# A gated linear attention with a maxout FFN: state products in one matmul, sums in quarters, a shorter weight conversion, and new orders

## The chip, the cores and the metric

The kernel runs on one core of one Trainium2 chip. The metric is device time in microseconds (us): the median of the timed runs. A profile of one execution gives a span, from the first to the last instruction. Engines are called as in the profile: PE is TensorE (matmul), PEld its weight loads, DVE VectorE, ACT ScalarE, POOL GpSimd, SP SyncE, which issues most DMAs.

## What is computed

Attention with a complex, data-dependent decay per step, then a feed-forward layer that takes the maximum of three products. Batch 4, 8 heads, 768 steps, head size 48; model width 384, inner width 768; 3072 tokens.

```python
mag = np.sqrt(a_re * a_re + a_im * a_im)
scale = np.minimum(mag, 0.999) / (mag + 1e-06)
a_re_n, a_im_n = (a_re * scale, a_im * scale)
for t in range(S):                                  # S_re, S_im: (B, H, 48, 48)
    new_re = ar * S_re - ai * S_im
    new_im = ar * S_im + ai * S_re
    kv = np.einsum('bhd,bhe->bhde', k[:, :, t], v[:, :, t])
    S_re, S_im = (new_re + kv, new_im)
    y[:, :, t] = np.einsum('bhd,bhde->bhe', q[:, :, t], S_re)
x = y.transpose(0, 2, 1, 3).reshape(3072, 384)
h = np.maximum(np.maximum(x @ w1, x @ w2), x @ w3)
out = h @ w_out
```

q, k, v, a_re and a_im are float32; the four weights are float64 and are turned into float32 on the chip.

## The kernel before

Steps are cut into 24 chunks x of 128 steps of one batch entry; a group g is two chunks (x and y in the lists' names) of two batch entries, 12 groups in all. A chunk is split again into two halves of 64 steps, and heads into odd and even ones, so that head 2i+j stands in partition half j.

The recurrence is solved without a loop over steps. The decay's logarithm (Ln, 128x768 per group) and its angle in turns (w) are formed elementwise by gates (ACT and DVE, some adds by DMA on POOL's queue). Per chunk and on PE: sums are running sums of Ln, cs running sums of the turns, F decays at cut points. ACT turns them into factors (Ek, Eq, En from sums; CS, cosine and sine, from cs; f from F). DVE multiplies k and q by them into uk and uq: per head, 48 cosine rows, a gap of 16, 48 sine rows, 112 in all. PE transposes both (tp), ACT or DVE copies them to K and Q, DVE makes rescaled copies (Q1, Q2, KB, QB, QG), and PE forms the scores A and B, which DVE and ACT pick into atm through masks. dk is the chunk's product of uk with v, which carries the state on (g); y sums atm with v and QG with the state, and is copied to xhx.

The FFN of a group: up multiplies xhx with two 384x768 weights from which w1 was taken off beforehand, so that a maximum with zero and a further maximum give h. The output product is done as seven products of half size (P1 to P7, sums S1 to S4 by DVE; r1, r6, r5, r7, r57, ox, oy add up the result ot), with Px and Py for the part that went through w1. Group 0 has a plain form of its own (up_one, O, o).

Order is written out by hand. SCHEDULE (lines 21 to 125) is a list of steps name:group; the kernel's Bound objects (line 210, the line of nearly every instruction in the profile) chain each engine's instructions in the order in which the list emits them. So each engine works strictly in list order, and what one engine does never changes the order on another. SLOTS names for each PSUM tile one of four slots (0, 2, 4, 6, two banks each); a tile waits for the last reader of its slot's former tile. OTHER holds the steps that go to their second engine: K and Q copies, xhx<-y, absolute values, and relu to DVE instead of ACT.

The parts that the change and the prediction touch:

- weight_step converts one of twelve 128x768 blocks of a weight. The high words of the float64 are read with a step of two. Step a (ACT) takes their absolute value scaled by 2^-112, b (DVE) caps it, c (DVE) shifts it by 3 bits, e (DVE) adds the low word's top 3 bits, f (DVE) puts the sign back in and writes the weight. g takes w1 off, by a DMA or on DVE.
- angles: cs, t, nf, af, sa, sb. cs has four matmuls of 128 rows and 64 weight columns, 192 moving columns, per chunk.
- state: dk has, for each of 8 heads n and half j, a matmul with weight columns 0 to 63 and one with 64 to 111; 64 rows, 48 moving columns. The last chunks of a batch entry do half of the heads.
- seven: r5 and r7 both add to yl: xr = yl + product 5, yl = yl + product 7.
- product: T and t transpose w1 (wt), M multiplies it with w_out (wm); w1 thus becomes part of the output weight. M0 to M2 come before the first up of group 0.

A float32 matmul shows as two records on PE and two weight loads, a transpose as one.

Of the kernel before, what the change touches and what calls it, by code (L numbers as in the profile page):

```python
# [26 lines left out]
turn1:0 Lry:1 sqr:1 t1:0 WL11:0 Lkx:0 tx:0 nfx:0 Wa11:0 Wb10:0 csy:0 afx:0 sax:0 mkx:0 Wb11:0 Wc10:0 Lix:1 sbx:0
uqx:0 sqi:1 Lix:2 Wc11:0 Lky:0 tpqx:0 ty:0 add:1 f3x:0 f2x:0 ukx:0 Fy:0 Qcx:0 We10:0 Wf10:0 nfy:0 tpkx:0 We11:0
lnL:1 WL2:0 Q2x:0 kEnx:0 Eqy:0 expe:1 Eky:0 relu:1 xor:1 expw:1 QBx:0 Kcx:0 abs:1 T2:0 T0:0 t0:0 CL:0 KBx:0 WL1:0
Wa1:0 pw:1 Q1x:0 mky:0 Wb1:0 f0y:0 f1y:0 Wc1:0 t2:0 f2y:0 Wf11:0 lne:1 Lnop:1 Ax:0 g0x:0 Lry:2 g1x:0 We1:0 g2x:0  # L30
half:1 Lqy:0 Cdx:0 f3y:0 Liy:2 Lvx:0 mqy:0 Wa2:0 Wb2:0 lnw:1 expL:1 M0:0 mulw:1 Wc2:0 M1:0 mulai:1 dkx:0 Wf1:0
stt:1 afy:0 say:0 sby:0 Wg1:0 sqi:2 WL4:0 Wa4:0 g3x:0 sumsx:1 Lrx:2 Cdy:0 sqr:2 M2:0 We2:0 QGx:0 atan:1 Wb4:0 Wf2:0
Lvy:0 Eqx:1 Enx:1 Ekx:1 uky:0 Zg:0 tpky:0 h1x:0 m0:0 m1:0 Lkx:2 Z3:0 Wg2:0 Wc4:0 uqy:0 tpqy:0 Lqx:1 Kcy:0 Qcy:0
Bx:0 b0x:0 turn:1 b1x:0 h2x:0 mqx:1 Fx:1 f0x:1 We4:0 f1x:1 Wf4:0 f2x:1 add:2 csx:1 tx:1 yx:0 KBy:0 Q2y:0 nfx:1 xx:0
h3x:0 f3x:1 lnL:2 expe:2 Q1y:0 WL5:0 Wa5:0 Lkx:1 sumsy:1 csy:1 Eky:1 ty:1 Ay:0 kEny:0 Wb5:0 WL7:0 relu:2 mkx:1
g0y:0 Wc5:0 expw:2 U01x:0 nfy:1 abs:2 u01x:0 Lvy:1 We5:0 Eqy:1 Z2:0 g1y:0 Wa7:0 QBy:0 afy:1 Wf5:0 Eny:1 g2y:0 g3y:0
Wb7:0 Wg4:0 U11x:0 xor:2 By:0 dky:0 U02x:0 Lvx:1 b1y:0 h1y:0 b0y:0 QGy:0 yy:0 addw:2 lnw:2 expL:2 xy:0 U11y:0 Wg5:0
u02x:0 U02y:0 afx:1 half:2 u11x:0 Wc7:0 lne:2 We7:0 mulw:2 mulai:2 sbx:1 h2y:0 Z4:0 sax:1 h3y:0 stt:2 atan:2 Wf7:0
U12x:0 u12x:0 say:1 sby:1 Cdy:1 WL8:0 Cdx:1 turn:2 ukx:1 uqx:1 U01y:0 u01y:0 u11y:0 Wa8:0 U12y:0 csy:2 ty:2 u12y:0
csx:2 tpqx:1 tx:2 u02y:0 Qcx:1 nfy:2 Lnop:2 nfx:2 tpkx:1 Fy:1 kEnx:1 Wb8:0 Wc8:0 We8:0 Kcx:1 Wg7:0 Wf8:0 U21y:0  # L40
Wg8:0 KBx:1 f0y:1 u21y:0 Lky:1 Lqy:1 mky:1 afy:2 sumsx:2 dkx:1 Q1x:1 f1y:1 f2y:1 f3y:1 Enx:2 U21x:0 u21x:0 afx:2
# [5 lines left out]
uky:2 Ekx:3 h2y:1 Eqx:3 Enx:3 yy:1 xy:1 Fy:2 f3y:2 h3y:1 dkx:2 f2y:2 abs:3 KBx:2 h0x:2 h1x:2 Q1x:2 f0y:2 f1y:2
U11:1 u11:1 tpky:2 Kcy:2 Lky:3 QBx:2 QGx:2 addw:3 Lqx:3 h2x:2 mqx:3 h3x:2 xor:3 half:3 Cdx:2 tpqy:2 Qcy:2 Q2x:2
lnw:3 kEny:2 expL:3 sumsy:3 Eqy:3 Q2y:2 Eny:3 Lkx:3 mkx:3 Fx:3 Eky:3 U01:1 Ax:2 Q1y:2 J1:0 mulw:3 mulai:3 g0x:2
g1x:2 u01:1 Cdy:2 f3x:3 f2x:3 g2x:2 g3x:2 J2:0 Bx:2 f0x:3 Dx:0 f1x:3 Dy:0 stt:3 KBy:2 h0x:3 U12:1 b0x:2 b1x:2 u12:1  # L50
S3:1 Lvy:2 yx:2 U02:1 QBy:2 Lvx:3 Lry:4 atan:3 turn:3 Liy:4 csy:3 csx:3 Lix:4 Lrx:4 sqr:4 sqi:4 add:4 lnL:4 ty:3
xx:2 By:2 u02:1 Ay:2 S1:1 nfy:3 relu:4 tx:3 expe:4 S2:1 expw:4 P5:1 P6:1 g0y:2 afy:3 say:3 sby:3 nfx:3 sbx:3 g1y:2
afx:3 sax:3 abs:4 dky:2 P1:1 Lqy:3 g2y:2 g3y:2 b1y:2 J4:0 QGy:2 P7:1 Px:1 P2:1 b0y:2 h0y:2 h1y:2 ukx:3 tpkx:3 lne:4
Lnop:4 r1:1 Liy:5 mky:3 h2y:2 h3y:2 S4:1 Kcx:3 uqx:3 yy:2 Lqx:4 kEnx:3 mqy:3 tpqx:3 Qcx:3 P3:1 r6:1 xy:2 Py:1 r5:1
r7:1 P4:1 Fy:3 uky:3 r57:1 f0y:3 f1y:3 xor:4 half:4 oy:1 ox:1 Q1x:3 addw:4 dkx:3 h1x:3 Lvy:3 f2y:3 f3y:3 h0y:3
h2x:3 sumsx:4 Ekx:4 h3x:3 lnw:4 QGx:3 expL:4 Eqx:4 Fx:4 KBx:3 U11:2 Dx:1 QBx:3 mulai:4 Q2x:3 f2x:4 Enx:4 u11:2
Cdy:3 Lkx:4 f1x:4 f0x:4 U01:2 uqy:3 f3x:4 mulw:4 stt:4 atan:4 tpky:3 Kcy:3 Ax:3 g0x:3 mqx:4 g1x:3 Bx:3 g2x:3 g3x:3
b1x:3 b0x:3 u01:2 Cdx:3 turn:4 U02:2 Lrx:5 u02:2 mkx:4 kEny:3 csy:4 csx:4 tx:4 nfx:4 ty:4 nfy:4 yx:3 xx:3 sumsy:4
KBy:3 Eqy:4 Eky:4 Lry:5 S3:2 Eny:4 sqr:5 dky:3 h1y:3 h2y:3 h3y:3 tpqy:3 Qcy:3 Q2y:3 Lix:5 sqi:5 Px:2 afy:4 add:5
lnL:5 expe:5 Dy:1 U12:2 u12:2 S1:2 Py:2 P7:2 Q1y:3 relu:5 lne:5 QBy:3 afx:4 P4:2 Ay:3 By:3 expw:5 S2:2 g0y:3 sbx:4  # L60
abs:5 g1y:3 sax:4 QGy:3 ukx:4 uqx:4 P6:2 P5:2 S4:2 g2y:3 g3y:3 P2:2 P1:2 Lqy:4 r1:2 Liy:6 mqy:4 b1y:3 P3:2 b0y:3
r6:2 r5:2 r7:2 tpkx:4 r57:2 ox:2 oy:2 kEnx:4 tpqx:4 yy:3 xy:3 Fy:4 say:4 Lky:4 sby:4 mky:4 uky:4 Lnop:5 Kcx:4 uqy:4
sumsx:5 xor:5 half:5 U11:3 KBx:4 addw:5 lnw:5 expL:5 mulw:5 Lqx:5 mulai:5 Cdx:4 h0x:4 f2y:4 stt:5 f3y:4 Ekx:5 f0y:4
Lkx:5 Dy:2 Dx:2 Qcx:4 Enx:5 Q1x:4 Cdy:4 u11:3 Eqx:5 QBx:4 mkx:5 Lry:6 QGx:4 Lvx:4 U01:3 Lix:6 atan:5 Q2x:4 u01:3
f1y:4 h0y:4 U02:3 Lrx:6 u02:3 sqr:6 dkx:4 h1x:4 sqi:6 h2x:4 h3x:4 Fx:5 f0x:5 f3x:5 add:6 f1x:5 f2x:5 Ax:4 g0x:4
Lqy:5 g1x:4 Bx:4 lnL:6 expe:6 g2x:4 g3x:4 U12:3 lne:6 b1x:4 tpky:4 turn:5 mqx:5 b0x:4 tpqy:4 Qcy:4 u12:3 Lvy:4
# [5 lines left out]
f1y:5 lnw:6 Lqx:6 h0y:5 u11:4 Q2x:5 expL:6 mulai:6 mulw:6 U01:4 u01:4 tpky:5 h0x:5 Eqx:6 Kcy:5 tpqy:5 stt:6 Ax:5
Lix:7 atan:6 g0x:5 Qcy:5 g1x:5 g2x:5 Bx:5 kEny:5 g3x:5 b0x:5 Q2y:5 U02:4 sqi:7 b1x:5 add:7 lnL:7 relu:7 expe:7
u02:4 U12:4 Fx:6 f2x:6 S3:4 f3x:6 half:6 turn:6 f0x:6 u12:4 Lvy:5 dky:5 h1y:5 Q1y:5 f1x:6 sumsy:6 dkx:5 Eny:6 csy:6
csx:6 h1x:5 mqx:6 S1:4 Dy:3 ty:6 nfy:6 S2:4 Eqy:6 Lqy:6 mqy:6 Eky:6 P1:4 KBy:5 tx:6 nfx:6 afx:6 lne:7 expw:7 afy:6
P7:4 abs:7 Lky:6 Ay:5 QBy:5 g0y:5 g1y:5 g2y:5 yx:5 g3y:5 addw:7 sbx:6 sax:6 ukx:6 uqx:6 By:5 say:6 P5:4 xx:5 P6:4
r1:4 r6:4 r5:4 lnw:7 xor:7 S4:4 half:7 Px:4 P2:4 b0y:5 Py:4 r7:4 P4:4 r57:4 P3:4 expL:7 mulw:7 QGy:5 oy:4 tpqx:6
tpkx:6 b1y:5 Lnop:7 mky:6 Qcx:6 Q1x:6 ox:4 Liy:8 kEnx:6 yy:5 sumsx:7 xy:5 Cdx:6 Enx:7 Fy:6 f2y:6 f0y:6 f3y:6
mulai:7 f1y:6 Eqx:7 QBx:6 QGx:6 Q2x:6 stt:7 Lqx:7 Ekx:7 Lix:8 U01:5 sqi:8 Lry:8 Cdy:6 Kcx:6 Lrx:8 Lvx:6 dkx:6 h1x:6
sby:6 mqx:7 h2x:6 h3x:6 uqy:6 uky:6 sqr:8 add:8 Dy:4 atan:7 turn:7 Ax:6 g0x:6 lnL:8 Lkx:7 expe:8 xor:8 g1x:6 relu:8  # L80
# [962 lines left out]
```

## Time and profile before

| what | value |
|---|---|
| median of 3 runs | 561.72 us (558.76 to 562.83) |
| span of the profiled execution, its only time on record | 556.9 us |
| PE busy | 524.6 us, 94%, 10086 records |
| PEld busy | 449.0 us, 81% |
| DVE busy | 490.4 us, 88%, 770 instructions |
| ACT busy | 370.0 us, 66%, of it 45 table loads 57.7 us |
| POOL busy | 74.4 us, 13% |
| DMA | 49.09 MB, mean 88 GB/s |
| mean granted TensorE clock | 0.988 |

The costliest groups on PE by busy time are up (177.4 us, 792 records), y (39.4 and 38.4), the output products, A (31.6) and dk (25.2 for the 64-column and 22.8 for the 48-column matmuls). Matmuls overlap, so a group's busy time is not what it adds to the span; the chain of waits, which follows the work that ended last, shows that better, with 34% of the span in up, 7% in y, 5% in A and 4% in dk. In the profile's slices a digit is the busy share of an engine in one fortieth of the span, in tenths. A window's row gives busy time by engine with the number of instructions, then the granted clock, the DMA share and GB/s. A group's row gives the engine, the operation, out<-in, the tile of the array where it is one (rows*columns), shapes and count, then busy time, the mean duration in ns, and the idle time in front of it.

### The profile page before, as it was taken

How to read it: one execution, taken by the hardware profiler on the slowest of the kernel's cores; microseconds unless marked ns; L12 is line 12 of the kernel's file. 1: busy time of each engine (PE TensorE's matmuls, PEld its weight loads, DVE VectorE, ACT ScalarE, POOL GpSimd, SP SyncE). 2: the span in 40 equal slices, each digit the busy share in tenths (PEclk: the TensorE clock that was granted, in tenths of full speed). 3: DMA queues.
4: the chain of work that ended last, by engine and by line, in shares of the span. 5: the costliest groups of instructions: out<-in, count | busy, mean ns of one | idle time of the engine just before them, and what ended most of it. 6: DMA issues, size and time to landing. Idle time of an engine off the chain costs nothing.

```text
span 556.9 us, 22739 instructions
## 1 busy us (share of the span) xinstructions
PE 524.6 (94%) x10086; PEld 449.0 (81%) x10086; DVE 490.4 (88%) x770; ACT 370.0 (66%) x652; POOL 74.4 (13%) x117
## 2 busy tenths in 40 slices
PE   1669799989999999999999999999999999999997
PEld 0356588778888898888988888988888888998986
DVE  5999999989998899999988897999999999886524
ACT  5999989867965867787766858777646855530100
POOL 8105250002030001000120200120010020000000
PEclk9869999999999999999999999999999999999999
DMA  8977976456055164235364136542361144000000
GB/s 218 287 191 156 206 154 102 78 105 123 18 108 109 21 123 77 48 63 92 68 115 82 33 61 121 110 88 50 58 126 31 32 88 82 10 31 2 7 25 29
DMA packets 142530, 49.09 MB, mean 88 GB/s; under 512 B 130528, under 2 KB 135648, under 8 KB 142432
## 3 DMA queue, kind: packets, MB, share of 16 engines
q1 hardware_dynamic: 136272, 37.77, 31.9%
q0 software_dynamic: 6160, 9.87, 10.4%
q8 instruction: 79, 1.29, 1.0%
q14 instruction: 19, 0.16, 0.1%
HBM read 33.03 MB, written 4.72 MB: 68 GB/s over the span
## 4 chain that ended last, share of the span: by engine, by line
PE 84%; DVE 6%; DMA 4%; SPq 2%; issue 1%; ACT 1%; POOL 0%; DVEq 0%
PE up L210 34%; PE op L210 24%; PE y L210 7%; PE A L210 5%; PE tp L210 4%; PE dk L210 4%; PE sums L210 3%; PE cs L210 2%; SPq L210 2%; DMA xhx<-in_moe_w_out_dram 2%; PE F L210 2%; DVE xhx L210 1%; PE B L210 1%; DMA k<-in_k_dram 1%; DMA ar<-nf 1%
## 5 line engine op out<-in xcount | busy, mean ns | idle before, releaser
L210 PE MATMUL up<-xhx,w 128*128 128x256 f32 x792 | 177.4, 382 | 0.1
L210 PEld LDWEIGHTS up<-xhx,w 128*128 128x128 f32 x792 | 148.6, 190 | 21.5 <-PE B L210 0.3
L210 ACT ACT_TABLE_LOAD x45 | 57.7, 1283 | 1.5 <-PEq L1027 0.8
L210 ACT COPY atm<-B 32x128 f32<-32x128 f32 x96 | 24.5, 255 | 36.9 <-DVE atm L210 22.9
L210 PE MATMUL op<-wo,xhx 128*128 128x192 f32 (+1 forms) x220 | 48.5, 364 | 0.0
L210 DVE TENSOR_TENSOR Q<-Q,f 112x1024 f32<-112x1024 f32 (+1 forms) x48 | 45.4, 950 | 0.8 <-ACT Q L210 0.6
L210 ACT ACTIVATE f<-F 48x232 f32<-48x232 f32 x96 | 34.4, 359 | 13.2 <-PE F L210 5.4
L210 POOL DMA_DIRECT2D ar<-nf x40 | 34.2, 1280 | 65.3 <-DVE ar L210 54.7
L210 PE MATMUL y<-atm,vb 128*32 128x64 f32 x1152 | 39.4, 221 | 1.4 <-issue 1.1
L210 PEld LDWEIGHTS op<-wo,xhx 128*128 128x128 f32 x220 | 36.5, 190 | 4.3 <-DVE q L210 0.3
L210 POOL DMA_DIRECT2D Ln<-e x11 | 11.1, 1005 | 214.6 <-ACT e L210 53.9
L210 PE MATMUL y<-QG,g 112*32 112x64 f32 x1408 | 38.4, 219 | 0.9 <-issue 0.8
L210 PEld LDWEIGHTS y<-atm,vb 128*32 128x32 f32 x1152 | 32.5, 109 | 6.4 <-issue 3.6
L210 PEld LDWEIGHTS y<-QG,g 112*32 112x32 f32 x1408 | 34.8, 109 | 1.3 <-issue 1.0
L210 DVE TENSOR_TENSOR ot<-ot,op 128x192 f32<-128x192 f32 (+1 forms) x67 | 27.1, 413 | 9.0 <-PE op L210 4.3
L210 PE MATMUL op<-wo,strassen 128*128 128x192 f32 x176 | 33.0, 331 | 0.0
L210 PE MATMUL A<-Q,K 112*32 112x80 f32 x1536 | 31.6, 234 | 1.3 <-DVE Q L210 1.3
L210 DVE COPY_PREDICATED atm<-masko,A 128x256 f32<-128x256 uint8 x72 | 31.2, 435 | 1.6
L210 PE MATMUL op<-w,strassen 128*128 128x192 f32 x176 | 32.5, 329 | 0.0
L210 PEld LDWEIGHTS A<-Q,K 112*32 112x32 f32 x1536 | 27.2, 110 | 5.0 <-issue 1.9
L210 ACT COPY Q<-tp 112x1024 f32<-112x1024 f32 x23 | 23.3, 1013 | 10.3 <-PE tp L210 10.0
L210 ACT COPY ot<-op 128x192 f32<-128x192 f32 (+1 forms) x13 | 4.5, 342 | 38.2 <-PE op L210 38.2
(151 smaller groups left out, 1120.8 us busy)
## 6 DMA issues: line engine op xcount, KB each, us to landing
ar<-in_a_re_dram SPq DMA_DIRECT2D x24, 192.0 KB, 3.7
ai<-in_a_im_dram SPq DMA_DIRECT2D x24, 192.0 KB, 3.8
q<-in_q_dram SPq DMA_DIRECT2D x96, 48.0 KB, 2.6
k<-in_k_dram SPq DMA_DIRECT2D x96, 48.0 KB, 2.9
...
```

Of the source, the lines that this page charges most:

```text
L210: ins = f(*a, **kw)
```

## The change

- Weight conversion: five steps instead of six. b comes first and clamps the signed high word on DVE (two operations in one instruction, read with a step of two, written packed); a is Prelu on ACT in place, with a slope for negative numbers that turns the sign into a bit beyond the shift; c shifts; e adds the low bits and writes the weight. f is gone.
- cs: eight matmuls of 32 weight columns instead of four of 64.
- dk: one matmul of 112 weight columns instead of 64 and 48.
- r5 and r7 become r75, one DVE instruction over both halves, with yl read twice.
- Three ACT biases are numbers instead of columns of a tile.
- Tiles from rotating pools become fixed pairs chosen by chunk; Ek and Eq no longer share theirs.
- SCHEDULE, SLOTS and OTHER are new throughout. On POOL the late constants (CL) move to the front.

```diff
-        if step == "a":
-            activation(out=ex.bitcast(FP), in_=high.bitcast(FP), func=AF.Abs, scale=2.0 ** -112)
-        elif step == "b":
-            dve.tensor_single_scalar(out=ex.bitcast(FP), in_=ex.bitcast(FP), scalar=LAST, op=OP.min)
+        if step == "b":
+            dve.tensor_scalar(out=ex.bitcast(FP), in0=high.bitcast(FP), scalar1=LAST, scalar2=-LAST, op0=OP.min,
+                              op1=OP.max)
+        elif step == "a":
+            activation(out=ex.bitcast(FP), in_=ex.bitcast(FP), func=AF.Prelu, alpha=-2.0 ** 32,
+                       scale=-2.0 ** -112 if i in (0, 3, 6) else 2.0 ** -112)
         elif step == "c":
-            if i in (0, 3, 6):
-                dve.tensor_scalar(out=ex, in0=ex, scalar1=3, scalar2=-0x80000000, op0=OP.logical_shift_left,
-                                  op1=OP.bitwise_or)
-            else:
-                dve.tensor_single_scalar(out=ex, in_=ex, scalar=3, op=OP.logical_shift_left)
+            dve.tensor_single_scalar(out=ex, in_=ex, scalar=3, op=OP.logical_shift_left)
         elif step == "e":
-            dve.scalar_tensor_tensor(out=ex, in0=low, scalar=29, in1=ex, op0=OP.logical_shift_right, op1=OP.bitwise_or)
-        elif step == "f":
-            dve.scalar_tensor_tensor(out=dst.bitcast(I32), in0=high, scalar=-0x80000000, in1=ex,
-                                     op0=OP.bitwise_and, op1=OP.bitwise_xor)
+            dve.scalar_tensor_tensor(out=dst.bitcast(I32), in0=low, scalar=29, in1=ex, op0=OP.logical_shift_right,
+                                     op1=OP.bitwise_or)
...
-                activation(out=e, in_=e, func=AF.Ln, scale=1e-6 * math.exp(-LNMAX), bias=least)
+                activation(out=e, in_=e, func=AF.Ln, scale=1e-6 * math.exp(-LNMAX), bias=math.exp(-LNMAX))
...
             for ch in range(2):
-                for j in range(2):
-                    dst, m = ps[j * L64:(j + 1) * L64, ch * HC:(ch + 1) * HC], slice(ch * L64, (ch + 1) * L64)
-                    mm(out=dst, lhsT=upto[:, m], rhs=every(T["w", g][:, c * DM:(c + 1) * DM], j), start=True, stop=True)
+                for o in (0, L64, 32, L64 + 32):
+                    j, m = o // L64, slice(ch * L64 + o % L64, ch * L64 + o % L64 + 32)
+                    mm(out=ps[o:o + 32, ch * HC:(ch + 1) * HC], lhsT=upto[:, m],
+                       rhs=every(T["w", g][:, c * DM:(c + 1) * DM], j), start=True, stop=True)
...
-            E = T[name, x] = nat2.tile([P, DM], FP, tag=name[:1 + (n == 1)], name=name[:1 + (n == 1)])
+            E = T[name, x] = es[name][c]
...
-                    for lo, hi in ((0, L64), (L64, DD)):
-                        mm(out=ps[lo:hi, j, n * D:(n + 1) * D], lhsT=both(T["Uk", x], n)[r, lo:hi],
-                           rhs=T["v", x][r, ch, i, j * D:(j + 1) * D], start=True, stop=True)
+                    mm(out=ps[0:DD, j, n * D:(n + 1) * D], lhsT=both(T["Uk", x], n)[r],
+                       rhs=T["v", x][r, ch, i, j * D:(j + 1) * D], start=True, stop=True)
...
-                out, in0, in1 = {"r6": (yl, xl, r.get(6)), "r5": (xr, yl, r.get(5)), "r7": (yl, yl, r.get(7)),
+                if name == "r75":
+                    two_ = ot.rearrange("p c n -> p (c n)")[:, NH:3 * NH].rearrange("p (u n) -> p u n", u=2)
+                    again = yl.rearrange("p (u n) -> p u n", u=1).to_broadcast([P, 2, NH])
+                    dve.tensor_tensor(out=two_, in0=again, in1=ps[:, 1, 0:DM].rearrange("p (u n) -> p u n", u=2), op=OP.add)
+                    return
```

The head of the lists, where the engines' orders differ first (before, then after):

```diff
-Lrx:0 Lix:0 sqi0:0 WL0:0 sqr0:0 xor0:0 add0:0 Wa0:0 Wb0:0 Wc0:0 We0:0 Liy:0 Wf0:0 lnL0:0 expw0:0 expe0:0 relu0:0
+Lrx:0 sqr0:0 Lix:0 sqi0:0 add0:0 lnL0:0 expe0:0 Zf:0 CL:0 expw0:0 lne0:0 relu0:0 WL0:0 Wb0:0 xor0:0 Lnop0:0 Lry:0
```

More of the change, by code (lines that the diff above doesn't have):

```diff
@@ L27 @@
[L27 to L41, printed above, removed]
@@ L47 @@
[L47 to L61, printed above, removed]
@@ L62 @@
[L62 to L66, printed above, removed]
@@ L72 @@
[L72 to L76, printed above, removed]
@@ L77 @@
[L77 to L80, printed above, removed]
-g2x:6 mkx:7 U11:5 KBx:6 u11:5 g3x:6 U12:5 u01:5 lne:8 U02:5 u12:5 S3:5 Lnop:8 u02:5 Bx:6 b0x:6 b1x:6 tpky:6 tpqy:6
@@ new lines @@
+g3x:0 lnL:1 expe:1 expw:1 relu:1 abs:1 pw:1 We10:0 xor:1 Wb1:0 Eky:0 Wa11:0 Wc11:0 Wa1:0 Eqy:0 lne:1 f0y:0 half:1 Lix:2
+Lky:0 WL4:0 Lrx:2 kEnx:0 Wc1:0 We11:0 Wb2:0 We1:0 KBx:0 Eny:0 t2:0 f1y:0 Wa2:0 f2y:0 Wc2:0 We2:0 lnw:1 expL:1 mulai:1
+mulw:1 Wb4:0 mqy:0 stt:1 Cdy:0 Lnop:1 Cdx:0 afy:0 sby:0 Wa4:0 sqr:2 atan:1 say:0 f3y:0 mky:0 Wc4:0 QBx:0 Liy:2 WL5:0
+sqi:2 turn:1 uky:0 Wb5:0 Wg1:0 M0:0 M1:0 M2:0 Wg2:0 Zg:0 Z3:0 uqy:0 Wa5:0 Wc5:0 m0:0 Bx:0 m1:0 add:2 We4:0 We5:0 Lqy:1
+WL7:0 Lky:1 WL8:0 Liy:3 Lix:3 Lqx:1 Wg4:0 Z4:0 Z2:0 Wg5:0 b1x:0 tpqy:0 tpky:0 Qcy:0 Kcy:0 csx:1 dkx:0 h1x:0 tx:1 b0x:0
@@ new lines @@
+sumsx:1 yx:0 Q2y:0 QBy:0 nfx:1 Q1y:0 xor:2 Enx:1 Ekx:1 Eqx:1 csy:1 Ay:0 lnL:2 ty:1 xx:0 h2x:0 nfy:1 mkx:1 KBy:0 h3x:0
+U01x:0 U11x:0 U02x:0 expw:2 expe:2 relu:2 abs:2 lne:2 u11x:0 u01x:0 afx:1 g0y:0 g1y:0 g2y:0 Wb7:0 g3y:0 Wa7:0 kEny:0
+half:2 u02x:0 QGy:0 Wc7:0 mqx:1 By:0 Fx:1 sumsy:1 b1y:0 b0y:0 f3x:1 dky:0 h1y:0 yy:0 f2x:1 f1x:1 f0x:1 addw:2 lnw:2
+Eqy:1 expL:2 Eny:1 Cdx:1 Cdy:1 We7:0 h2y:0 Wg7:0 Lnop:2 xy:0 h0x:1 h3y:0 Eky:1 U12x:0 mulw:2 mulai:2 stt:2 u12x:0 Wb8:0
+U11y:0 U01y:0 U02y:0 U12y:0 sax:1 atan:2 turn:2 u01y:0 u02y:0 U21y:0 U21x:0 sbx:1 sby:1 Wa8:0 u11y:0 u21x:0 Wc8:0 We8:0
@@ new lines @@
+dky:3 tpqx:4 u12:2 h1y:3 h2y:3 Qcx:4 h3y:3 yy:3 S1:2 xy:3 S3:2 csy:4 expw:5 abs:5 ty:4 Kcx:4 xor:5 KBx:4 S2:2 Q1x:4
+mqy:4 Lnop:5 addw:5 QGx:4 half:5 Q2x:4 kEnx:4 P1:2 r1:2 P5:2 mky:4 S4:2 Px:2 Py:2 P2:2 U01:3 P4:2 lnw:5 expL:5 u01:3
+P6:2 P7:2 P3:2 mulai:5 mulw:5 nfy:4 Cdy:4 Cdx:4 sqi:6 afy:4 sby:4 say:4 QBx:4 r6:2 r75:2 stt:5 r57:2 oy:2 uqy:4 uky:4
+ox:2 atan:5 turn:5 U11:3 U02:3 u02:3 csy:5 u11:3 sqr:6 add:6 ty:5 nfy:5 csx:5 tx:5 nfx:5 Lkx:5 Dx:2 Lqy:5 Lvx:4 Lvx:5
+Dy:2 Lry:7 Ax:4 g0x:4 g1x:4 g2x:4 g3x:4 Fy:4 Fx:5 dkx:4 U12:3 h1x:4 lnL:6 f3y:4 relu:6 h2x:4 h3x:4 f2y:4 expw:6 f1x:5
@@ new lines @@
+mqy:5 U01:4 u01:4 uky:5 kEnx:5 Q2x:5 U11:4 f3y:5 f0y:5 atan:6 f2y:5 f1y:5 sqi:7 add:7 u11:4 dkx:5 tpky:5 h1x:5 h0y:5
+kEny:5 Q1x:5 half:6 uqy:5 turn:6 QGx:5 U02:4 KBx:5 u02:4 lnL:7 expe:7 Kcy:5 U12:4 tpqy:5 dky:5 f0x:6 f1x:6 lne:7 f3x:6
+f2x:6 Qcy:5 S3:4 u12:4 xor:7 S1:4 csx:6 tx:6 nfx:6 h1y:5 Ax:5 csy:6 Bx:5 afx:6 g0x:5 sbx:6 expw:7 relu:7 Q2y:5 S2:4
+g1x:5 g2x:5 KBy:5 g3x:5 ty:6 b1x:5 Q1y:5 nfy:6 QBy:5 P5:4 S4:4 abs:7 P1:4 afy:6 Dx:3 Lrx:8 P7:4 P6:4 b0x:5 Lkx:6 Lqy:6
+Liy:8 Lky:6 Lix:8 Lry:8 Lqx:6 Lvx:6 Dy:3 sumsx:6 By:5 yx:5 Ekx:6 Enx:6 Eqx:6 xx:5 sby:6 r1:4 Ay:5 g0y:5 QGy:5 g1y:5 Py:4
@@ new lines @@
+P4:4 Px:4 P2:4 Lnop:7 addw:7 sax:6 say:6 P3:4 lnw:7 mqx:6 g2y:5 g3y:5 b0y:5 b1y:5 half:7 r6:4 Cdy:6 Cdx:6 r75:4 r57:4
+mkx:6 oy:4 ox:4 uqx:6 ukx:6 sumsy:6 Fy:6 yy:5 Eky:6 Eqy:6 expL:7 Eny:6 f3y:6 tpqx:6 tpkx:6 mqy:6 xy:5 Qcx:6 sqr:8 mky:6
+mulw:7 mulai:7 stt:7 QGx:6 uqy:6 f2y:6 sqi:8 atan:7 U01:5 uky:6 u01:5 Q2x:6 QBx:6 U11:5 Kcx:6 f1y:6 turn:7 Q1x:6 add:8
+kEnx:6 f0y:6 u11:5 lnL:8 relu:8 KBx:6 U12:5 u12:5 tpky:6 tpqy:6 dkx:6 Kcy:6 h1x:6 Qcy:6 csy:7 csx:7 tx:7 expw:8 expe:8
+h2x:6 h3x:6 Bx:6 Ax:6 abs:8 ty:7 xor:8 nfx:7 g0x:6 sbx:7 g1x:6 g2x:6 g3x:6 b1x:6 b0x:6 half:8 S3:5 nfy:7 Q1y:6 U02:5
@@ new lines @@
+turn:8 Q2x:7 h0x:7 f3y:7 f1y:7 f0y:7 f2y:7 u11:6 csy:8 csx:8 Ax:7 sqi:9 ty:8 nfy:8 g0x:7 afy:8 g1x:7 g2x:7 QBx:7 add:9
+lnL:9 tx:8 h0y:7 Q2y:7 g3x:7 kEnx:7 xor:9 U12:6 U01:6 Q1y:7 nfx:8 kEny:7 QGx:7 KBx:7 u12:6 u01:6 U02:6 u02:6 Lqy:8 Lkx:8
+Lky:8 Lrx:10 Lry:10 Dx:5 Lvx:8 Lqx:8 Lvy:8 Dy:5 dkx:7 dky:7 h1x:7 h2x:7 h3x:7 relu:9 h1y:7 h2y:7 h3y:7 Fx:8 expw:9 f2x:8
+f0x:8 f1x:8 f3x:8 sumsx:8 sumsy:8 Ekx:8 Eqx:8 Enx:8 Ay:7 Bx:7 Eky:8 b1x:7 P1:6 r1:6 Eny:8 b0x:7 expe:9 Eqy:8 S1:6 P5:6
+S2:6 S3:6 P6:6 P7:6 KBy:7 g0y:7 g1y:7 g2y:7 mqx:8 abs:9 say:8 addw:9 yx:7 r6:6 g3y:7 QBy:7 S4:6 mky:8 By:7 half:9 QGy:7
@@ L181 @@
     TWOPI = 6.283185
[L182 removed]
+    LAST = float(np.array(0x47EFFFFF, dtype=np.int32).view(np.float32))
     SUMS, ADDS = 2, 1
@@ L268 @@
     ident = const.tile([P, P], FP, name="ident")
-    biases = const.tile([P, 4], FP, name="biases")
-    for i, b in enumerate((-0.5 * math.pi, LNMAX, math.exp(-LNMAX))):
-        dve.memset(biases[:, i:i + 1], b)
-    hpi, lnmax, least = (biases[:, i:i + 1] for i in range(3))
+    biases = const.tile([P, 1], FP, name="biases")
+    dve.memset(biases, 1.0)
     def keep(view, base, pattern, mult):
@@ L311, with two_of @@
     KB = const.tile([P, 2 * H, 32], FP, name="KB")
+    def two_of(nm, *shape):
+        return [const.tile([P, *shape], FP, name="%s%d" % (nm, i)) for i in range(2)]
+    kqs = {nm: two_of(nm, 2, 4, D) for nm in "kq"}
+    turned = {nm: two_of(nm, DM) for nm in ("t", "nf")}
+    css = two_of("CS", H, 2, D)
+    lns = two_of("Ln", W)
+    es = {nm: two_of(nm, DM) for nm in ("Ek", "Eq", "En")}
+    Ks, Qs = two_of("K", H, P), two_of("Q", 4 * H, 80)
+    ots = const.tile([P, C, DM], FP, name="ot")
     def constants_early():
@@ L542, in gates @@
         elif name == "relu":
-            once(("Ln", g), lambda: nat2.tile([P, W], FP, tag="Ln", name="Ln"))
+            T["Ln", g] = lns[g % 2]
             if other():
@@ L546, in gates @@
             else:
-                activation(out=part("Ln") if g >= ADDS else L, in_=L, func=AF.Relu, scale=-0.5, bias=lnmax)
+                activation(out=part("Ln") if g >= ADDS else L, in_=L, func=AF.Relu, scale=-0.5, bias=LNMAX)
         elif name == "Lnop":
@@ L609, in angles @@
         elif name == "af":
-            T["af", x] = nat2.tile([P, DM], FP, tag="t", name="af")
+            T["af", x] = turned["t"][c]
             magnitude(T["af", x], T["nf", x])
         elif name in ("sa", "sb"):
-            CS = once(("CS", x), lambda: nat2.tile([P, H, 2, D], FP, tag="CS", name="CS"))
+            CS = T["CS", x] = css[c]
             if name == "sa":
-                activation(out=CS[:, :, 0], in_=hv(T["af", x]), func=AF.Sin, scale=TWOPI, bias=hpi)
+                activation(out=CS[:, :, 0], in_=hv(T["af", x]), func=AF.Sin, scale=TWOPI, bias=-0.5 * math.pi)
             else:
@@ L922, in seven @@
         else:
-            ot = [once(("ot", g * C + c), lambda: fp2.tile([P, DM], FP, tag="ot", name="ot")) for c in range(C)]
-            xl, xr, yl, yr = (ot[c][:, h * NH:(h + 1) * NH] for c in range(C) for h in range(2))
+            ot = ots
+            xl, xr, yl, yr = (ot[:, c, h * NH:(h + 1) * NH] for c in range(C) for h in range(2))
             if name == "r1":
@@ L942, in project @@
         elif name == "o":
-            T["ot", x] = fp2.tile([P, DM], FP, tag="ot", name="ot")
-            act.copy(out=T["ot", x], in_=T["op", x])
+            act.copy(out=ots[:, x % C], in_=T["op", x])
         elif name == "D":
```

167 lines of the change are left out of this document (87 added, 80 removed).

## The prediction

> **What bounds the kernel now.** I read the page first: busy time by engine, then the 40 slices.
>
> ```profile
> PE 524.6 (94%) x10086; PEld 449.0 (81%) x10086; DVE 490.4 (88%) x770; ACT 370.0 (66%) x652; POOL 74.4 (13%) x117
> PE   1669799989999999999999999999999999999997
> DVE  5999999989998899999988897999999999886524
> ACT  5999989867965867787766858777646855530100
> ```
>
> DVE is full from the second slice on, PE only from about the ninth. So I split the span in two windows (columns: PE, PEld, DVE, ACT, POOL).
>
> ```profile
> 0.00:122.00 122.00, 94.36 (x1851) 69.33 (x1851) 113.08 (x182) 105.49 (x189) 34.41 (x69) 0.94 0.75 166
> 122.00:550.00 428.00, 426.89 (x8218) 376.57 (x8218) 375.46 (x583) 264.49 (x464) 40.01 (x48) 1.00 0.35 66
> ```
>
> After 122 us PE is busy 426.9 of 428 us: it is the bound, and DVE and ACT have 53 and 164 us to spare. Before that DVE (113 of 122) and ACT feed it. PE's busy time includes overlap, so I added the work itself: every PE group of the list at the pitch of its unbroken records (216 ns for 256 columns, 162.5 for 192; a set of four 32-column tiles of A 69 ns), plus the price of changes of tile shape below. That gives 513.0 us. PE's clock less the work done before it is 37.8 us at the first up of group 1 (121.9 us) and 40.2 at the last (538.9): the sum follows the trace over 417 us within 2.4. So the time is PE's work plus about 38 us of waiting in the first 122.
>
> The chain of waits, in order of time, shows two prices (start, length, what):
>
> ```profile
> 145.62 1.15 PE A L210 x64
> ...
> 172.73 1.24 PE A L210 x64
> 174.27 4.08 PE up L210 x18
> 178.35 1.45 PE cs L210 x16
> ...
> 185.01 3.88 PE up L210 x18
> ...
> 311.74 1.07 PE dk L210 x57
> ```
>
> A costs 1.15 when a group of its own tile shape follows and 1.24 when not; up 3.88 against 4.08. Where the shape of the array's tiles changes, PE empties and the first weights load in the open.
>
> The weight loads, with the shape of the weights behind the tile (PEld groups, shapes kept apart, mean ns):
>
> ```profile
> L210 PEld LDWEIGHTS up<-xhx,w 128*128 128x128 f32 x792 | 148.6, 190 | 21.5 <-PE B L210 0.3 <-issue 0.3 <-DVE k L210 0.3
> L210 PEld LDWEIGHTS A<-Q,K 112*32 112x32 f32 x1536 | 27.2, 110 | 5.0 <-issue 1.9 <-DVE Q L210 1.6 <-ACT E L210 0.3
> L210 PEld LDWEIGHTS dk<-vb,uk 64*64 64x64 f32 x704 | 22.9, 135 | 3.3 <-issue 1.8 <-ACT Q L210 0.5 <-DVE KB L210 0.3
> L210 PEld LDWEIGHTS dk<-vb,uk 64*48 64x48 f32 x704 | 20.4, 119 | 0.3 <-issue 0.3
> L210 PEld LDWEIGHTS tp<-ident,uk 64*112 64x112 f32 x384 | 12.9, 133 | 3.7 <-issue 2.1 <-ACT wo L210 0.5 <-DVE ot L210 0.5
> ```
>
> 32, 48, 64 and 128 columns take 110, 119, 135, 190 ns: 83 plus 0.83 per column. Only the transposes (tp) load 112 columns in 133, half the slope.
>
> **The change part by part.**
>
> State products (dk): the term that decides. Two matmuls of 64 and 48 weight columns become one of 112; 704 become 352, each two records. Records of one 64-column tile of dk stand 58 ns apart: 64 x 0.83 + 5, although 48 moving columns need only 40. The same law fits F (48 columns: 45 ns), B (32: 32 ns) and up<-xT (128: 112 ns), so these groups wait for weight loads, and the tiles load side by side. For 112 columns it gives 93 + 5 = 98 ns per pair of row tiles. A full set has 16 turns: 16 x 58.3 = 0.93 us before, 16 x 98.3 = 1.57 after. 352 matmuls are 22 full sets: +0.64 x 22 = **+14.1**. All of it lies on PE's path. The bounds: the transposes' slope allows 52 ns a turn (0.83 us a set, -2.2), their moving floor scaled to 48 columns 43 ns (0.69, -5.3); if the two row tiles loaded in turn, 192 ns (+47). I take the law, as four widths of ordinary matmuls lie on it and only transposes off it.
> [...]
>
> Changes of tile shape: cs in quarters has the shape of A, B and y (128x32), dk now that of tp (64x128). By the instruction lists PE changes shape 190 times before, 152 after. Into the full array 61 and 46, at 0.20 (4.08 - 3.88); into 128x32 51 and 45, at 0.12 (1.24 - 1.15, and 0.03 of first load); into 64x64 39 and 27, at 0.13 (F); into 64x128 27 and 35, at 0.14 (32 tp records 1.04, unbroken 0.90); into 128x64 13 and 0, at 0.15 (cs 1.45, unbroken 1.30). 29.1 less 23.0, and dk's wider first load 14 x 0.045: **-5.5**. Between -4.5 and -7.
>
> Cosine turns' sums (cs) themselves: 8 records of two tiles (pairs 163 ns apart) become 16 of four; A shows four tiles abreast at the same rate per column, so 4 x 163 both times. 0; at most 8 more records x 7 ns x 24 = +1.3.
>
> Weight conversion, 12 blocks: the last DVE step goes (0.95, in a queue 0.87), the clamp now reads every second word (0.55 as before, or up to the 0.95 of the other strided steps), Abs (0.91) becomes Prelu on packed data (ACT 768: 0.84). DVE -5.6 to -10.4, ACT -0.8, all in the first 80 us; DVE now comes first, so a block crosses DVE-ACT-DVE. Joined sums: 22 x 0.35 become 11 x 0.55, -1.7 on DVE, hidden under PE after 122 us. Biases as numbers: 0.09 on 40 ACT instructions, -3.6; two more table loads, +2.6. Moves between DVE and ACT (K and Q copies, xhx<-y, af, relu): 6 us of rows each way, net under 1. Separate E tiles and fixed buffers only loosen reuse; no DMA is added (SP 373, POOL 117 instructions both times). All queues are in a new order: on SP the four loads of k for chunk 0 (192 KB) now stand ahead of weight blocks 3, 6, 10 and 9, whose clamp on DVE waits for the landing itself, with ordinary DVE work behind it; at the 325 GB/s of 10 to 20 us that is 0.6 us later, held in the small waits below. On POOL the late constants (7.9 us of rows) go ahead of the first adding DMAs instead of between them; POOL is busy 74 of 557 us. Outside the start all this is 0: cover is PE's 100%; were PE to fall under DVE's 375 us of 428, it would show.
>
> The start: by the lists, ACT's work up to the last copy of the turned weights (uk<-wt) is 36.1 us before, ended at 42.9; after it is 35.4, so 42.2, and the wm products can follow, which in the list no longer wait for another chunk of scores. PE's own work ahead of them is 13.8: its lag is 28.4. PEclk falls to half in the trace when PE idles (25 to 35 us), and PE would idle here too: +2 for the first matmuls, 30.4. From there the lists put DVE 6 to 16 us of work ahead of PE at equal places (before: 17 to 28); with DVE's own lag of 11 to 14 us, it is ready at 28 or less, so PE does not wait again. 37.8 becomes about 31.8 with 1.4 for small waits: **-6**. Between 0 (a new wait in its place) and -9.
>
> Sum, against this execution's span of 556.9: +14.1 - 5.5 - 6 = 559.5. The median of the runs, 561.7, stands 4.8 above the span: **564**.
>
> **The rivals.**
> (1) Faster: dk is priced by its number. For it: a turn of tp, same tile and 112 columns, takes 56 ns. Against it: the 0.83 slope of all ordinary loads. dk then gains 2.2 to 5.3 instead of losing 14.1: about **546**. A turn under 76 ns is enough for 1% faster.
> [...]
> (2) Slower: the start keeps its 37.8 us, because DVE, in order, stands behind a conversion step that waits for ACT (clamp, Prelu, shift), with the turns' arithmetic queued behind it. For it: ACT is busy 29 of 30 us from 10 to 40. Against: DVE has 6 to 10 us less to do there. 564 + 6 = **570**; it decides if PE's lag at the first up of group 1 is above 36.
> (3) Slower: the row tiles' weights load one after the other: +33 more, **597**. Against it: tp pairs at 56 ns with loads of some 50 each.
>
> **How the numbers follow.** Forecast 0.62 (564, own range 557 to 571 from the ends of the start and shape terms), rival 1 0.15, rival 2 0.17, rival 3 0.06. About 1% (5.6 us) is what a measurement of this kernel can tell from no change. Faster by more: rival 1 and 0.03 of the forecast, 0.18; within: 0.45 of the forecast and 0.02 of rival 2, 0.47; slower: the rest, 0.35. Eight in ten reaches from rival 1's centre, 546, to 573, and leaves out rival 3.
>
> **What would show it.** dk: one LDWEIGHTS group 64x112 at about 175 ns mean (133 would be rival 1), a full set about 1.7 us in the chain. cs sets about 1.3 where A, B or y follow. PE's lag at the first up of group 1 near 31. DVE busy 482, fewer DVE groups xhx<-w. Wrong: a dk set under 1.1 us, or PE idle by more than 3 us after 122.

## The result, and the profile after

The changed kernel takes **614.05 us** (median of 4 runs, 607.18 to 616.89) against 561.19 for the kernel before on the same chip (558.76 to 562.83): a ratio of 1.0865, 95% interval 1.0779 to 1.0950; two of the four runs, 616.38 and 616.89, are over 1.5% above the fastest, and the ratio leaves them out. The forecast was 564, with 546 to 573 as its range. The profiled execution took 607.18 us, its span is 605.5. Run again later (e17 below), the kernel took 614.13 (606.85 to 615.61).

Busy time and slices of the changed kernel:

```profile
PE 550.5 (91%) x9574; PEld 473.1 (78%) x9574; DVE 478.4 (79%) x751; ACT 368.3 (61%) x648; POOL 73.6 (12%) x117
PE   3669899997999999899999889999999999899996
PEclk9679999999899999899999979999999999989999
```

PE has holes all along the span, and its granted clock falls with them (mean 0.962, before 0.988). The stretch in which PE was busy 426.9 of 428 us before (columns as there):

```profile
122.00:550.00 428.00, 406.03 (x7327) 357.59 (x7320) 352.32 (x542) 264.06 (x459) 38.57 (x46) 0.97 0.33 64
```

PE now stands still for 22 us of it, and DVE does less in the same time than before (352 for 375), so no engine is busy throughout. PE's waits from 122 to 600 us, the six largest of 17 (what waited, for what; us in total, times, longest):

```profile
PE op L201 <- ACT ot L201: 7.0, 5, 3.2
PE tp L201 <- DVE ot L201: 3.4, 2, 2.2
PE B L201 <- issue: 3.2, 1, 3.2
PE y L201 <- issue: 3.0, 3, 1.1
PE tp L201 <- ACT atm L201: 2.1, 1, 2.1
PE op L201 <- DVE ot L201: 1.7, 3, 0.6
```

The same view of the kernel before has one row in all:

```profile
PE y L210 <- issue: 0.8, 1, 0.8
```

And the term that the forecast hung on: the weight loads of dk, and full sets of dk and cs in the chain of waits of the changed kernel:

```profile
L201 PEld LDWEIGHTS dk<-vb,uk 64*112 64x112 f32 x704 | 37.2, 177 | 4.1 <-issue 2.9 <-ACT K L201 0.6 <-ACT Q L201 0.5
```
```profile
165.73 1.59 PE dk L201 x32
...
226.58 1.44 PE cs L201 x32
```

The loads take 177 ns for a forecast of about 175, and a set of dk 1.59 us for the 1.57 of the sum. In PE's records this set of cs takes 1.32 us from its start to the start of the next group, A, for a forecast of about 1.3 (the chain's 1.44 runs to the end of its last record). The prices were right, and the time was not.

**Where the 48.6 us between the two profiled spans are.** PE's own work, summed over the new list at the prices of the prediction, is 521.7 us for 513.0: +8.7. Most of the rest is waiting, in three kinds, each measured in the trace of PE's records. *Waits for another engine*: gaps of over 0.2 us that end with that engine's work. *Waits for instructions* ("issue" in the profile): gaps of over 0.2 us inside a group or ahead of one, where nothing else is late; what they are is shown by e12 and e13. Three gaps that the profile calls "issue" are not of this kind, as they lie at no block end (explained under e12): e3 has one of 1.3 us and e5 one of 1.9, counted in the first kind, and e16 has one of 4.0, not counted. *Half clock*: time at a granted clock of 0.50 in PE's span, times one half (an upper bound, as PE stands still for a part of it).

| kernel | span less 556.9 | PE's own work | waits for engines | for instructions | half clock |
|---|---|---|---|---|---|
| before, whole span | | 513.0 | 15.2 | 1.9 | 6.8 |
| after, more than before | +48.6 | +8.7 | +16.8 | +6.3 | +15.3 |
| e2, dk joined in the old lists | +24.0 | +17.2 | -1.9 | +4.0 | +6.8 |
| e6, cs in quarters in the old lists | +13.7 | -1.3 | 0 | +9.9 | +1.7 |
| e5, conversion in the old lists | +12.5 | 0 | +3.9 | +4.3 | +6.8 |
| e3, these three in the old lists | +31.6 | +15.9 | +2.2 | +7.3 | +8.5 |
| e1, after with dk split again | +59.4 | -4.3 | +22.9 | +21.9 | +11.9 |

The rows below the first are differences from the kernel before. Their terms miss the span's difference by 1.5 to 7 us, as the half clock is an upper bound and smaller gaps are left out. (In e2 dk has the shape of tp while cs keeps its 128x64: by the prices 3.1 us of changes of shape on top of the 14.1.)

### The profile page after: what moved, and what is told of

Same layout as the page of the kernel before. It is cut to its first block, busy times and chain, and to the rows that moved or that the text cites. A ratio compares the mean times of both kernels' runs of the same rounds, so it can differ in the third digit from the quotient of the medians.

```text
span 605.5 us, 21649 instructions
## 1 busy us (share of the span) xinstructions
PE 550.5 (91%) x9574; PEld 473.1 (78%) x9574; DVE 478.4 (79%) x751; ACT 368.3 (61%) x648; POOL 73.6 (12%) x117
## 4 chain that ended last, share of the span: by engine, by line
PE 66%; DVE 14%; ACT 6%; DMA 5%; SPq 5%; issue 4%; POOL 0%; DVEq 0%; ACTq 0%
PE up L201 27%; PE op L201 16%; PE dk L201 6%; SPq L201 5%; PE y L201 5%; PE tp L201 3%; PE A L201 3%; DVE atm L201 2%; PE cs L201 2%; DVE g L201 2%; PE F L201 2%; DVE Q L201 1%; DVE ot L201 1%; DMA Ln<-e 1%; PE sums L201 1%
## 5 line engine op out<-in xcount | busy, mean ns | idle before, releaser
L201 DVE TENSOR_TENSOR Q<-Q,f 112x512 f32<-112x512 f32 (+1 forms) x48 | 45.2, 952 | 9.1 <-ACT f L201 9.0
L201 POOL DMA_DIRECT2D ar<-nf x40 | 37.6, 1313 | 117.8 <-DVE ar L201 65.3
L201 DVE TENSOR_TENSOR ot<-ot,op 128x384 f32<-128x384 f32 (+1 forms) x56 | 25.6, 465 | 29.0 <-PE op L201 12.5
L201 ACT ACTIVATE xhx<-up 128x768 f32<-128x768 f32 x18 | 14.6, 809 | 50.4 <-PE up L201 47.0
L201 PE MATMUL y<-QG,g 112*32 112x64 f32 x1408 | 41.8, 227 | 2.4 <-issue 2.0
L201 PE MATMUL dk<-vb,uk 64*112 64x48 f32 x704 | 39.6, 262 | 1.3 <-issue 0.9
L201 PEld LDWEIGHTS dk<-vb,uk 64*112 64x112 f32 x704 | 37.2, 177 | 4.1 <-issue 2.9
L201 DVE TENSOR_TENSOR xhx<-xhx,up 128x768 f32<-128x768 f32 x22 | 20.9, 951 | 21.6 <-PE up L201 21.5
L201 PEld LDWEIGHTS op<-wo,strassen 128*128 128x128 f32 x176 | 29.9, 195 | 6.3 <-ACT ot L201 5.0
L201 PEld LDWEIGHTS op<-w,strassen 128*128 128x128 f32 x176 | 30.7, 199 | 4.9 <-ACT ot L201 3.5
```

Source lines behind the costliest of these rows:

```text
L201: ins = f(*a, **kw)
```

## The experiments

Times are medians beside runs of the kernel before on the same chip: 558.0 for e1 to e4, 561.2 for e5 to e8, 560.9 for e9 and e11 to e13, 559.8 for e14 to e17. The theories, as the expectations number them: **1** the new lists wait by themselves (1a: from SP's order of loads, 1b: from the engines' lists; 1c: DVE is a link, 1d: it is not); **2** the lists would hold, and the waits are the longer dk passed on; **3** one of the edits brings the waits itself (**4** the conversion, **4b** cs); **5** PE's blocks of instructions; **6** single places in the new lists; **7** the landing of one weight block in the start.

**e1: the changed kernel, dk split again.**

```diff
-                    mm(out=ps[0:DD, j, n * D:(n + 1) * D], lhsT=both(T["Uk", x], n)[r],
+                    for lo, hi in ((0, L64), (L64, DD)):
+                        mm(out=ps[lo:hi, j, n * D:(n + 1) * D], lhsT=both(T["Uk", x], n)[r, lo:hi],
```

> The changed kernel with one part undone: dk again as two matmuls of 64 and 48 weight columns; lists, slots and all else as changed. Theory 1 (the new lists wait more by themselves, dk costs only its own 22 sets x 0.64 us): 614 - 14 + about 1 for changed tile shapes, 599 to 603; PE's lag behind its own work still grows by 30 us or more after 122 us. Theory 2 (the lists would hold with the short dk, and the waits are the longer dk passed on): the growth goes with it, 555 to 572.

617.86 (615.61 to 621.49): 13 us less work on PE, and no time won. Neither number came. Theory 2 falls: with the short dk PE waits for other engines no less (22.9 us more than before, 16.8 with the long dk). The reason why theory 1's 599 did not come either is in the table: beside these waits, 15.6 us more of "issue".

**e2: the kernel before, dk joined** (the same edit the other way).

> The kernel before with one part of the change: dk as one matmul of 112 weight columns, lists and all else as before. Theory 1 (dk costs its own work, wherever it stands): 561 + 14, less 0 to 2 for tile shapes that now equal those of tp: 573 to 576. Theory 2 (a longer dk is passed on as waits): 585 or more. Rival that dk's price is not real work but overlap in the records: 561 to 564.

582.59 (581.65 to 582.99), +24.6 for 17.2 of work. Between the theories: beyond the work there are 4 us of issue and up to 7 of half clock, and not one wait for another engine after 122 us.

**e3: the old lists with conversion, cs and dk of the change** (W steps renamed in place: a to b, b to a, f to e).

> The kernel before, in its own lists, slots and buffers, with three edits of the change put in place: conversion in five steps, cs in quarters, dk joined (joined sums r75 and the numbers as biases are left out). Theory 1 (the lists are the cause): 561 + 14 for dk - 2 to 4 for shapes, conversion 0 to -5: 566 to 574, and after less this, some 40 to 48 us, is the price of the lists. Theory 3 (one of the edits itself brings the waits): 595 or more. Theory 2: between, 580 to 595.

590.20 (587.67 to 590.61), 32.2 more than the kernel before beside it. That is above theory 1's 566 to 574, by issue and half clock, and in theory 2's range; but theory 1's main point holds. All of PE's waits from 122 us on in e3 are these,

```profile
PE F L207 <- issue: 2.4, 2, 1.2
PE tp L207 <- issue: 1.8, 1, 1.8
PE B L207 <- issue: 1.4, 2, 1.2
PE y L207 <- issue: 1.4, 2, 0.7
PE sums L207 <- issue: 0.7, 1, 0.7
```

with no engine among them. The same matmuls in the new lists have 17.7 us of waits for engines there. So the new lists cost about 21 us on top of the edits (52.9 less 32.2, each beside its own runs of the kernel before), half of the 40 to 48 expected. "Lists" means here all that came with them: the slots, the choice of second engines, the fixed buffers, the joined sums and the biases. None of these was tried alone.

**e4: k and q loads earlier in the new list** (for example Lkx:6, 108 words earlier).

```diff
-P6:4 b0x:5 Lkx:6 Lqy:6
+abs:6 ukx:5 Lkx:6 uqx:5
```

> The changed kernel, in whose list each load of k and q stands right behind the last reader of the buffer that it fills; nothing else moves, on SP these loads now stand ahead of the gate loads (ar, ai) that wait for their buffers. Theory 1a (the waits start on SP, in order: gate loads wait for late readers, and k and q queue behind them): 590 to 604, and k and q are no longer the last thing that DVE waits for. Theory 1b (the waits are on the engines' own lists, DVE, ACT and PE each close behind the other; SP is only seen beside them): 610 to 618.

632.72 (630.22 to 636.49), slower. In the start the moved loads wait for a buffer with weight blocks queued behind them on SP (the last w_out block went out at 41.12 instead of 29.98 us, and PE stood still for 11.88 us at 48). From the first up of group 1 to the last up, PE's lag (its clock less its own work so far) grows by 40.1 us, in the changed kernel by 38.1, and the same 3.2, 2.2 and 2.1 us of longest waits are there: the loads were not the cause. Theory 1a falls for the steady stretch, 1b stands.

**e5: conversion alone, e6: cs alone, in the old lists.**

> The kernel before, in its own lists, with the conversion in five steps (clamp in the place of the old first step, Prelu in the place of the old clamp, the last DVE step gone) and nothing else. Theory 4 (the lag of 48 us instead of 40 at the first up of group 1 with three edits in the old lists comes from the conversion: DVE-ACT-DVE crossing in lists made for ACT-DVE): 562 to 568, lag there 44 to 49. The prediction's view (6 to 10 us less on DVE in the start): 550 to 558, lag 30 to 38.

> The kernel before with cs in quarters and nothing else. By the prices of tile shapes (no 128x64 any more, 13 changes fewer into it, cs now of the shape of A, B and y): 2 to 4 us less PE work, 554 to 557 against 558. Theory 4b (cs, not the conversion, brought the extra lag): 562 or more.

570.33 (567.55 to 573.47) and 574.11 (572.45 to 577.77). The conversion makes DVE 9.6 us less busy (480.8 for 490.4) and costs 9: PE's lag at the first up of group 1 is 51.7 instead of 38.0, with DVE now waiting for ACT (w for L 3.4 us, for w 1.5; the clamped block for Prelu 2.3) and ACT for DVE's clamp (8.8 us in 5 waits) between 8 and 122 us, where the kernel before has one such wait of DVE, 2.7 us, and none of ACT for a clamp. Cs in quarters saves 1.3 us of work and costs 13, of which 9.9 are issue. In e5 the time and the lag lie above theory 4's ranges, but in its direction and by its mechanism; 4b came by its number, for another reason. The three parts cost 24.6, 9.1 and 12.9 alone and 32.2 together: a sum over parts does not describe them.

**e7, e8: 66 DVE sums added to the changed kernel and to the one before.**

```diff
+            if name == "uq" and g > 0:
+                many = ident.rearrange("p (a n) -> p a n", a=1).to_broadcast([P, 2, P])
+                for _ in range(3):
+                    dve.tensor_tensor(out=idle, in0=many, in1=many, op=OP.add)
```

> The changed kernel with work added on DVE alone: three sums of 128x256 into a tile that nobody reads, behind uq of every chunk from group 1 on, 22 x about 0.95 = 21 us. DVE stands idle for 63 of the 398 us from 122 to 520. Theory 1c (the new lists leave DVE's steps just in time, so that DVE in list order is a link of the chain of waits in most of it): 630 to 640. Theory 1d (the links are ACT, SP and PSUM slots, DVE has its idle time to give): 612 to 620.

> The kernel before with the same work added on DVE (21 us). DVE stands idle for 26 of the 358 us from 122 to 480, less than in the changed kernel. Theory 1c (what counts is how far DVE's steps lie ahead of PE's, 17 to 28 us in this list, not idle time): 558 to 566. If idle time counts: 575 or more, and more than the changed kernel loses.

637.97 (631.09 to 640.67) and 572.80 (571.22 to 573.68). DVE is busy 24.6 us longer in the new lists, and that costs 24 us; in the old ones it is busy 23.5 us longer, and that costs 11.6, though DVE has less idle time there. This speaks for theory 1c, but the old list is less well covered than its 558 to 566 said.

**e9: 66 ACT copies added to the changed kernel** (the same, act.copy behind sb).

> The changed kernel with work added on ACT alone: three copies of 128x256 into a tile that nobody reads, behind the sine of every chunk from group 1 on, 22 x about 0.9 = 20 us, where ACT stands idle for a third of the time. Theory 6 (PE waits for ACT and DVE at single places where their order is late, so added work is paid there in part): 620 to 632. If ACT's idle time covers it: 612 to 617.

626.92 (624.21 to 629.57): ACT is busy 25 us longer, and that costs 13. In the profiled executions 8.5 us of it lie between the first up of group 1 and the last up. ACT is a link too.

**e12, e13: the kernel before with 64 and with 256 more instructions on PE, ahead of its first step** (16 and 64 matmuls of one column; each is two records and two loads).

```diff
+    for _ in range(16):
+        mm(out=first[0:1, 0, 0:1], lhsT=biases[:, 0:1], rhs=biases[:, 0:1], start=True, stop=True)
```

> The kernel before with nothing changed but 16 products of one column and one row on PE ahead of its first step, while PE has nothing to do (64 instructions in PE's stream: each is two weight loads and two records). Theory 5 (PE's instructions come in blocks of 256 by DMA, about 3.2 us from one block's start to the next one's readiness; the old list stands so that block ends fall into long products, and any edit that changes the number of PE's instructions loses that): stalls of 14 to 19 us in groups of small tiles (now 1.9), more with half clock behind them, 573 to 590. Theory 1 (only the order of steps and their durations count): 557 to 563.

> The same with 64 such products, 256 instructions: block ends lie again where they lay. Theory 5: 557 to 564, like the kernel before. If the small products themselves cost the time: more than with 16.

577.42 (576.92 to 578.41, ratio 1.0314, 1.0263 to 1.0364) and 562.32 (558.65 to 562.63, ratio 1.0031, 1.0000 to 1.0062). PE is idle for 7 to 8 us between the small products and its first real one, so their own time costs nothing. Yet 64 instructions cost 16.5 us, and 256 cost nothing that can be told from the noise. PE's waits of e12 from 122 us on, the four largest, and all of e13:

```profile
PE B L210 <- issue: 4.4, 3, 1.6
PE dk L210 <- issue: 2.5, 2, 1.7
PE y L210 <- issue: 2.0, 2, 1.6
PE sums L210 <- issue: 1.9, 2, 1.1
```
```profile
PE y L210 <- issue: 0.9, 1, 0.9
```

So what costs is not the products but where the later instructions come to stand, and this repeats after 256. The page of the changed kernel lists the transfers themselves,

```profile
q8 instruction: 75, 1.23, 0.8%
```

75 packets of 16 KB for PE's 9574 records and as many loads, 255 instructions to a packet. If one numbers PE's instructions in the trace, the first one after such a stall is number 192 or 193 past a multiple of 256 in every kernel (with the three exceptions above): 1216, 1473, 4289, 8129, 9664 and 18624 in the changed one, 23 places in e1. The packet of a block starts 0.1 to 1.7 us after PE enters the block before it in 42 of 75 cases in the changed kernel and in 50 of 79 before (in the rest from 4.4 us ahead of that to 5.8 after), takes about 1 us, and at the stalls PE goes on 1.3 to 1.6 us after its end: as an estimate from these some 3.2 us, in which PE must have other instructions. A block holds 127 or 128 of PE's records with their loads: 127 of up take 27 us, but 127 of A, B or y can be through in 3 (64 of A take 1.15 to 1.24 us, 112 of y 1.72). In the old list block ends fall where PE is slow: moving them in the trace of before by 64 instructions, at 3.2 us a block, gives 14 to 15 us of stalls for under 0.5, and the run showed 15.3 for 1.9. At the six stalls of 0.9 us and more in the changed kernel the packet started later, 1.9 to 5.8 us after; so at the longest, with 0.97 of the DMA engines busy from 146 to 150 us:

```profile
147.69 0.22 PE B L201
147.91 3.18 issue
151.09 0.60 PE B L201 x27
151.74 2.13 PE A L201 x63
```

PE entered the block before at about 143, the packet started only at 148.57, and PE's clock then was 0.50 from 150.1 to 156.9 (A takes 2.13 for 1.11).

**e16: the changed kernel with the same 64 instructions.**

> The changed kernel with 16 products of one column on PE ahead of its first step (64 instructions). Theory 5 (its list, like the one before, stands so that ends of PE's blocks of 256 instructions fall into long products): about 13 us more stalls in groups of small tiles, 622 to 634. If the waits between engines hide them: 610 to 618.

622.78 (619.90 to 627.27), against 614.13 for the unchanged one on the same chip: +8.7, with stalls of 18.6 us for 8.2. Theory 5's range came: the new list, too, is one whose block ends mostly fall where PE is slow. So its own places of the block ends explain 6.3 of the 48.6 us, and some half clock behind them.

**e11: three words of the new list moved.**

```diff
-Eqx:5 b0x:4 Enx:5 r1:3
+r1:3 Eqx:5 b0x:4 Enx:5
-oy:5 g3y:6
+g3y:6 oy:5
-QGy:10 r57:9 oy:9 ox:9
+r57:9 oy:9 ox:9 QGy:10
```

> The changed kernel with three words of its list moved, and nothing else: r1 of group 3 ahead of three ACT steps (an exponential, a table change and two copies) behind which PE waits 3.20 us for it at 244.9; oy of group 5 behind the last pick of scores, which it holds up on DVE while PE waits 2.08 us at 349.7; QG behind oy and ox of group 9, 1.2 of the 2.19 us that PE waits at 530.0. Theory 6 (17 us of PE's waits after 122 us are single places in the new lists where one engine's order holds up another, each with some us of half clock behind it): 5.6 us of waits and 3 to 7 of half clock go, 601 to 606. If other steps come last at once in their place: 611 to 616.

609.88 (603.54 to 615.93), not clear as a time. Its profiled execution was the longest and lost 15 us more in the start, which the words do not touch; so I compare the growth of PE's lag from the first up of group 1 to the last up: 31.3 us for 38.1. The waits of 3.20, 2.08 and 2.19 us became 0.64, 1.53 and 1.64. In the changed kernel two of them look so in the chain:

```profile
244.15 0.49 ACT En L201
244.64 0.22 ACT ot L201
244.90 5.85 PE op L201 x24
...
347.68 0.56 DVE ot L201
348.24 0.35 DVE atm L201
...
349.72 1.11 PE tp L201 x32
350.83 2.25 PE dk L201 x32
353.08 1.72 PE tp L201 x32
```

ACT's copy ot (r1) stands behind the exponential En and more, though the product it reads had ended at 241.7. At 347.68 DVE's oy waited for PE, with the last pick of scores (atm), ACT's copies and PE's next tp behind it. What follows runs at half clock (0.50 from 351.5 to 358.3): dk 2.25 for 1.59, tp 1.72 for 1.04.

**e17, e14, e15: the changed kernel again, its start, and start and words together.**

```diff
-turn:1 uky:0 Wb5:0 Wg1:0 ... uqy:0 Wa5:0 Wc5:0 m0:0 ... We4:0 We5:0 Lqy:1 WL7:0 Lky:1 WL8:0
+turn:1 uky:0 Wg1:0 ... uqy:0 m0:0 ... We4:0 Wb5:0 Lqy:1 WL7:0 Lky:1 ... Kcy:0 Wa5:0 Wc5:0 We5:0 WL8:0 Wg5:0
```

> The changed kernel once more, as it is, on the chip of the next three. Theory 7 (its start depends on when one weight block lands, 38 us of lag when it is in time, 51 to 54 when not): 607 to 618, and the lag of the profiled execution is one of the two. If its first profile was the rule: 605 to 609.

> The changed kernel with the conversion of weight block 5 (its clamp, Prelu, shift and last step, and the load that waits for them) moved behind the copies of wm, Q and K of group 0 that stood behind its Prelu on ACT. Theory 7: the lag at the first up of group 1 stays at 36 to 42 us whenever the block lands, 603 to 609. If the full DMA queues of that stretch hold up something else as well: 610 to 618.

> The same start with the three words moved as well (r1 of group 3, oy of group 5, QG of group 10's first chunk pair): theories 6 and 7 together: 7 us less growth of the lag after the first up of group 1 than in the changed kernel, 596 to 603.

614.13 (606.85 to 615.61), 610.38 (607.04 to 615.46), 602.24 (599.96 to 605.11). The kernel itself comes out with a lag of 38.0 or 46.7 us at the first up of group 1. It varies, as theory 7 says, though 46.7 is not the 51 to 54 that it named. In e17 a weight block lands at 58.7 us and PE stands still for 4.8 us ahead of the transposes at 61, for a copy of wo on ACT. But e14's lag was 46.4: with the block moved, another landing came last, of ai at 57.7 us in its chain of waits. So theory 7's place is not the cause, or not the only one. What sets the start of the new list from one execution to the next stays open. e15's profiled span is 12.2 us shorter than e17's: its lag grew by 29.8 us for 35.9, and started from 40.6, which e14 does not explain. No version came near the kernel before.

## Why the prediction was wrong, step by step

**Right: the prices.** Dk's loads (177 ns for 175) and its sets (1.59 us for 1.57) came as worked out, and e2 bears the price out: of its 24.0 us, 17.2 are work by these prices, and the other 6.8 lie within its measured waits. PE's own work over the new list, 8.7 us more for the forecast's 14.1 - 5.5 = 8.6, is counted at the same prices, so it is no test of them; the changes of shape were not measured apart. (What decides there is the group ahead, not the one that follows: in the chain of before A takes 1.15 us behind B, of its own shape, at 145.62, and 1.24 behind tp at 172.73; up 3.88 behind op at 185.01, and 4.08 behind B at 174.27.) Rival 1 (loads of 133 ns, a set under 1.1 us) and rival 3 (a set of 3.07 us) are refuted by the same rows.

**The step that failed** is "Outside the start all this is 0: cover is PE's 100%", with "so PE does not wait again". PE's 100% was not a cover that any work could lie beside. It was a property of the old list: the order of its steps on DVE and ACT, and the places of its block ends. The new list lost the first, and a part of the second. From the first up of group 1 on, where the prediction had nothing but PE's work, PE's lag grew by 38 us (before: 1.3, or 2.4 as the prediction counted it): 17.7 of waits for engines, 6.1 for instructions, up to 11.9 of half clock behind them. What could have warned of it was in the prediction's own working: DVE's work lies 6 to 16 us ahead of PE's in the new list, 17 to 28 in the old. It set this against DVE's own lag of 11 to 14 us and took it as enough everywhere. But a single step behind a busy stretch can end last. E11 and e15 show three such places, worth some 6 to 7 us of lag, by their order alone; whether the other waits come from the order or from the slots and buffers that came with it was not tried.

**The start, -6, failed too**: the lag stayed at 38.0 in the profiled execution and was 46.7 in another. That is rival 2's condition (a lag above 36), and e5 shows its mechanism in the old lists, but its time, 570, was far off, as the main loss lay elsewhere.

**Missing altogether**: that the number of PE's instructions places the block ends. The change takes 16 matmuls (64 instructions) out of each full dk and puts 4 (16 instructions) into each cs. With e12, 64 instructions alone cost the old kernel 16.5 us; this is more than dk's 14.1, on which the whole forecast was decided. That the new list's block ends cost it only 6.3 us more was not foreseen either. The one place in the profile that hinted at it was the wait "PE y <- issue".

**The test stated for failure was right**: "PE idle by more than 3 us after 122" came out, by 22 us.
